# Sliding-window attention and ELU layer on one core: keys cast on load, the band added in PSUM, pairs 2 and 3 ahead of step 0

## The chip, the cores and the metric

The kernel runs on one core of one Trainium2 chip. The metric is the device time of one execution in microseconds: 305.26 us before the change, the median of three executions (304.96 to 305.6). The profiled execution spans 303.4 us, from the first to the last instruction. All times in the text are counted from that span's start.

A core has five engines that run side by side, each its own list of instructions in order: TensorE (PE, with its weight loads shown as PEld), VectorE (DVE), ScalarE (ACT), GpSimd (POOL) and SyncE (SP). POOL, ACT and SP also issue the transfers between memories.

## The reference

Attention over a window of 32 positions on each side, then a layer with ELU. The shapes are 8 batches, 8 heads, 576 positions, 64 values a head; the layer goes 512 to 2048 to 512 over 4608 tokens.

```python
def _attn_ref(q, k, v):
    scale = 1.0 / np.sqrt(D)
    scores = scale * np.matmul(q, k.transpose(0, 1, 3, 2))
    mask = np.abs(pos[:, None] - pos[None, :]) <= 32
    scores = np.where(mask, scores, -1000000000.0)
    scores = scores - np.max(scores, axis=-1, keepdims=True)
    attn = np.exp(scores)
    attn = attn / (np.sum(attn, axis=-1, keepdims=True) + 1e-09)
    return np.matmul(attn, v)

def _moe_ref(x, w_in, w_out):
    h = x @ w_in
    g = np.where(h > 0.0, h, np.exp(np.minimum(h, 0.0)) - 1.0)
    return g @ w_out
```

The attention's result, with the heads side by side, is `x`. Inputs and output are float32; the kernel works in bfloat16 with float32 sums.

## The kernel before

Attention goes by *pairs*: two blocks of 64 queries, all 8 heads, each block against 128 keys. There are 36 pairs. The layer goes by *steps*: 256 tokens by 256 of the 2048 hidden columns, 144 steps; step kk multiplies by `w_in` (`mm1`), takes the ELU, and multiplies by `w_out` (`mm2`) some steps later. Four pairs give the tokens of steps 0 to 7, and so on; from step 0 on, the pairs' work is put between the steps at fixed places.

Loads of the first batch. `load_qk` brings q or k as float32 over the queues of SP and ACT, and a cast to bfloat16 follows on VectorE. `load_cast` brings them over POOL's queue as bfloat16. Each half (HALF_A, HALF_B) has half of each head's positions in it.

```python
def load_qk(b, which, part, engs=(nc.sync, nc.sync)):
    t = lpool.tile([128, 2, nj * D], FP32, tag=f"f{which}{nj}", name=f"f{which}")
    ...
    for h in range(2):
        engs[h].dma_start(out=t[:, h, :], in_=src[:, :, h, :])

def load_cast(b, which, part):
    t = cpool.tile([128, 2, nj * D], BF16, tag=f"c{which}", name=f"c{which}")
    ...                                    # cpool has one buffer for each tag
    for h in range(2):
        nc.gpsimd.dma_start(out=t[:, h, :], in_=src[:, :, h, :])

def load_v(b, m):                          # block m of 128 keys, all heads, as bfloat16
    lo = 128 * m - WIN
    p0 = max(0, -lo)
    p1 = min(128, S - lo)
    nc.gpsimd.dma_start(
        out=V_e[b % 3][p0:p1, m, :, 0:D],
        in_=v[b, :, lo + p0:lo + p1, :].rearrange("h p d -> p h d"))

def rotate_v(b, m0, m1, parts=(0, 1)):     # V_o: the same rows, moved by 64
    e, o = V_e[b % 3], V_o[b % 3]
    for z in parts:
        nc.vector.tensor_copy(o[64 * z:64 * (z + 1), m0:m1],
                              e[64 * (1 - z):64 * (2 - z), m0 + z:m1 + z])

def load_w_in(c): ...                      # a quarter of w_in, POOL's queue
def load_w_out(c): ...                     # a quarter of w_out, POOL's queue
```

Quarter c of `w_in` serves four steps that use columns 512c to 512c+511. The attention of one pair:

```python
def scores(i, tag="s"):
    psS = ps_tile([128, 2, 512], FP32, tag, "psS")
    for z in range(2):
        ...
        for h in range(H):
            nc.tensor.matmul(
                psS[:, h % 2, hp * 128 + z * QB:hp * 128 + (z + 1) * QB],
                lhsT=kT[...], rhs=qT[...], start=True, stop=True)

def exponential(i):                        # ScalarE
    nc.scalar.activation(pu, psS, AX.Exp, scale=SCALE)

def mask(i):                               # VectorE
    nc.vector.tensor_mul(pm, pu, masks)    # masks: ones in the band, zeros outside

def pv(i): ...                             # 16 products pm x V_e or V_o
def normalize(i): ...                      # VectorE: reciprocal and product
def x_transpose(i): ...                    # TensorE
def x_evac(i, eng): ...                    # copy to xT
```

The start of the program (cut; `idle(n, tag)` is n matrix products of zeros, which fill TensorE's waits):

```python
for which in range(2):
    load_qk(0, which, HALF_A, (nc.sync, nc.scalar))
...
edges(0); edges(1)                         # VectorE memsets of the borders of V and k
masks = ...                                # POOL: memset and two selects
for m in (1, 0, 2):
    load_v(0, m)
...
for which in range(2):
    load_cast(0, which, HALF_B)
load_w_in(0)
...                                        # three more selects on masks
for m in (3, 4):
    load_v(0, m)
load_w_in(1)
load_w_out(0)
load_w_out(1)

idle(10, "y1")
front_cast(0, HALF_A, nc.vector)
front_transpose(0, HALF_A, nc.scalar, ("h0", "h1"))
idle(1, "u")
front_cast(1, HALF_A, nc.vector)
for (j0, n), tag, eng in zip(SPLIT, ("y0", "y1"), (nc.scalar, nc.vector)):
    transpose_qk(0, 1, HALF_A, j0, n, eng, tag)
idle(2, "h0")
for i, tag in ((0, "s"), (1, "u")):
    scores(i, tag)
    exponential(i)
idle(4, "y0")
rotate_v(0, 0, 2)
for i in (0, 1):
    mask(i)
pv(0)
front_transpose(0, HALF_B, nc.scalar, ("h0", "h1"))
pv(1)
for i in (0, 1):
    normalize(i)
x_transpose(0); x_evac(0, nc.scalar)
front_transpose(1, HALF_B, nc.vector, ("y0", "y1"))
x_transpose(1); x_evac(1, nc.scalar)
idle(3, "h1")
...                                        # loads of batch 1 and the other quarters
```

The steps. `psH` has two buffers, h0 and h1, so the `mm1` of step kk waits until the ELU of step kk-2 has read its buffer:

```python
def mm1(kk):
    ...                                    # 16 products into psum h0 or h1
    nc.scalar.activation(e_sb, ps, AX.Exp)
    if kk in (1, 2):
        nc.scalar.activation(m_sb, e_sb, AX.Copy, bias=-1.0)
    else:
        nc.vector.tensor_scalar(m_sb, e_sb, -1.0, None, ALU.add)

def elu(kk): ...                           # VectorE: g_sb = min(max(ps, 0), m_sb)

for kk in range(NSTEP + LAG):
    run(kk, "first")
    if 1 <= kk < NSTEP:
        elu(kk - 1)
    run(kk, "dve")
    if kk < NSTEP:
        mm1(kk)
    run(kk, "mid")
    for n in {2: (), 3: (), 4: (), 5: (2, 3)}.get(
            kk, (kk - LAG,) if kk >= LAG else ()):
        mm2(n)                             # cut: the last steps differ
    run(kk, "end")
```

Of the kernel before, what the change touches and what calls it, by code (L numbers as in the profile page):

```python
# [12 lines left out]
ALU = mybir.AluOpType  # L13
# [8 lines left out]
def kernel(  # L22
# [71 lines left out]
    def ps_tile(shape, dt, tag, name):  # L94
        return pools[tag].tile(shape, dt, tag=tag, name=name)
# [32 lines left out]
    def load_cast(b, which, part):  # L128
        z, nj = part
        t = cpool.tile([128, 2, nj * D], BF16, tag=f"c{which}",  # L130
                       name=f"c{which}")
        qk_c[b, which, z] = t
        src = (q, k)[which][b, :, z * NC * nj:(z + 1) * NC * nj, :].rearrange(
            "(g h) (c j) d -> c g h (j d)", h=2, j=nj)
        for h in range(2):
            nc.gpsimd.dma_start(out=t[:, h, :], in_=src[:, :, h, :])  # L136

    def load_v(b, m):
        lo = 128 * m - WIN
        p0 = max(0, -lo)  # L140
        p1 = min(128, S - lo)
        nc.gpsimd.dma_start(  # L142
            out=V_e[b % 3][p0:p1, m, :, 0:D],
            in_=v[b, :, lo + p0:lo + p1, :].rearrange("h p d -> p h d"))
# [28 lines left out]
    def load_w_in(c):  # L173
        w = D_FF // 4
        nc.gpsimd.dma_start(
            out=w_in_sb[:, :, c * w:(c + 1) * w],
            in_=moe_w_in[:, c * w:(c + 1) * w].rearrange(
                "(o p) f -> p o f", p=128))

    def load_w_out(c):  # L180
        n = NFO // 4
        nc.gpsimd.dma_start(
            out=w_out_sb[:, c * n:(c + 1) * n, :],
            in_=moe_w_out[c * n * 128:(c + 1) * n * 128, :].rearrange(
                "(o p) f -> p o f", p=128))
# [1 line left out]
    def w_in_at(c):  # L187
        return w_in_sb[0:1, 0, (c + 1) * (D_FF // 4) - 1:(c + 1) * (D_FF // 4)]

    for which in range(2):  # L190
        load_qk(0, which, HALF_A, (nc.sync, nc.scalar))

    zeros = cpool.tile([128, 512], BF16, name="zeros")
    nc.vector.memset(zeros, 0.0)  # L194
# [11 lines left out]
    make_identity(nc, ident)  # L206

    edges(0)
    edges(1)

    masks = cpool.tile([128, 5, QB], BF16, name="masks")
    nc.gpsimd.memset(masks, 1.0)
    nc.gpsimd.affine_select(
        out=masks, in_=masks, compare_op=ALU.is_ge, fill=0.0,
        base=0, pattern=[[0, 5], [-1, QB]], channel_multiplier=1)
    nc.gpsimd.affine_select(
        out=masks, in_=masks, compare_op=ALU.is_ge, fill=0.0,
        base=2 * WIN, pattern=[[0, 5], [1, QB]], channel_multiplier=-1)  # L220
    for m in (1, 0, 2):
        load_v(0, m)
    kinds = ["FE", "EE", "EL", "LF"]

    def kind(jb):
# [67 lines left out]
            later.append(evict)  # L293

    st = {}

    def scores(i, tag="s"):
        psS = ps_tile([128, 2, 512], FP32, tag, "psS")
        for z in range(2):
            jb = 2 * i + z  # L300
            b, qb = jb // NQB, jb % NQB
            for h in range(H):
                hp, base = h // 2, 64 * (h % 2)
                nc.tensor.matmul(  # L304
                    psS[:, h % 2, hp * 128 + z * QB:hp * 128 + (z + 1) * QB],
                    lhsT=kT[b % 2][base:base + 64, KPAD + hp * S + QB * qb - WIN:
                                   KPAD + hp * S + QB * qb - WIN + 128],
                    rhs=qT[b % 2][base:base + 64, hp, QB * qb:QB * (qb + 1)],
                    start=True, stop=True)
        st[i] = [psS, None, None, None, tag]  # L310

    def exponential(i):
        psS = st[i][0]
        pu = apool.tile([128, H, 2 * QB], BF16, tag="pu")
        nc.scalar.activation(  # L315
            pu, _bap(psS, [psS.ap[0], [1, 1024]]), AX.Exp, scale=SCALE)
        st[i][1] = pu

    def mask(i):
        psS, pu, _, _, _ = st[i]  # L320
        pm = apool.tile([128, H, 2 * QB], BF16, tag="pm")
        m0 = kinds.index(kind(2 * i) + kind(2 * i + 1))
        mm = masks[:, m0:m0 + 2, :]
        nc.vector.tensor_mul(  # L324
            pm, pu, _bap(mm, [mm.ap[0], [0, H], [1, 2 * QB]]))
        st[i][2] = pm
# [42 lines left out]
    def x_evac(i, eng=nc.vector):  # L369
        copy_on(eng, xT_of(i), st.pop(i))  # L370
# [12 lines left out]
    def front_cast(which, part, eng):  # L383
        for j0, n in SPLIT:
            cast_qk(0, which, part, j0, n, eng)

    def front_transpose(which, part, evac, tags, later=None):
        for (j0, n), tag in zip(SPLIT, tags):
            transpose_qk(0, which, part, j0, n, evac, tag, later)


    def idle(n, tag):
        ps = ps_tile([128, 512], FP32, tag, "ps_idle")
        for _ in range(n):
            nc.tensor.matmul(ps, lhsT=zeros[:, 0:128], rhs=zeros,  # L395
                             start=True, stop=True)
# [5 lines left out]

    for which in range(2):
        load_cast(0, which, HALF_B)
    load_w_in(0)
    for mi in (0, 4):
        nc.gpsimd.affine_select(
            out=masks[:, mi, :], in_=masks[:, mi, :], compare_op=ALU.is_ge,
            fill=0.0, base=-WIN, pattern=[[0, QB]], channel_multiplier=1)
    nc.gpsimd.affine_select(  # L410
        out=masks[:, 3, :], in_=masks[:, 3, :], compare_op=ALU.is_ge,
        fill=0.0, base=128 - WIN - 1, pattern=[[0, QB]],
        channel_multiplier=-1)
    for m in (3, 4):
        load_v(0, m)
    load_w_in(1)
    load_w_out(0)
    load_w_out(1)

    idle(10, "y1")  # L420
    front_cast(0, HALF_A, nc.vector)
    front_transpose(0, HALF_A, nc.scalar, ("h0", "h1"))
    idle(1, "u")
    front_cast(1, HALF_A, nc.vector)
    for (j0, n), tag, eng in zip(SPLIT, ("y0", "y1"), (nc.scalar, nc.vector)):
        transpose_qk(0, 1, HALF_A, j0, n, eng, tag)
    idle(2, "h0")
    for i, tag in ((0, "s"), (1, "u")):
        scores(i, tag)
        exponential(i)  # L430
    idle(4, "y0")
    rotate_v(0, 0, 2)
    for i in (0, 1):
        mask(i)
    pv(0)
    front_transpose(0, HALF_B, nc.scalar, ("h0", "h1"))
    pv(1)
    for i in (0, 1):
        normalize(i)
    x_transpose(0)  # L440
    x_evac(0, nc.scalar)
    front_transpose(1, HALF_B, nc.vector, ("y0", "y1"))
    x_transpose(1)
    x_evac(1, nc.scalar)
    idle(3, "h1")


    for which in range(2):
        load_cast(1, which, HALF_A)
# [32 lines left out]
        at(kk + 2, "end", x_evac, i, nc.scalar)  # L482


    at(0, "mid", scores, 2, "s")
    at(0, "mid", scores, 3, "u")
    for i in (2, 3):
        at(0, "mid", exponential, i)
    at(0, "mid", rotate_v, 0, 2, VS - 1, (0,))
    at(0, "mid", mask, 2)  # L490
    at(0, "mid", rotate_v, 0, 2, VS - 1, (1,))
    at(1, "dve", mask, 3)

    at(1, "mid", idle, 4, "y1")
    at(1, "mid", pv, 2)
    at(1, "mid", idle, 2, "y1")
    at(2, "dve", normalize, 2)
    at(2, "mid", pv, 3)
    at(2, "mid", normalize, 3)
    for i in (2, 3):  # L500
        at(3, "mid", x_transpose, i)
        at(3, "mid", x_evac, i, nc.scalar)
        at(3, "mid", lambda n: mm2(n), i - 2)
    at(4, "dve", swap_pools)

    for part, kq in ((HALF_A, 7), (HALF_B, 15)):
# [171 lines left out]
            mm1(kk)  # L678
        run(kk, "mid")

        for n in {2: (), 3: (), 4: (), 5: (2, 3)}.get(
                kk, (kk - LAG,) if kk >= LAG else ()):

            if n < NSTEP - 2:
                mm2(n)
            elif n == NSTEP - 1:
                mm2(n - 1, ((0, 0), (0, 1), (1, 0)))
                mm2(n, ((0, 0), (0, 1)))
                mm2(n - 1, ((1, 1),))
                mm2(n, ((1, 0), (1, 1)))  # L690
        run(kk, "end")
# [30 lines left out]
```

The softmax here doesn't subtract the row's maximum and nothing guards it: scores larger than these inputs give would overflow.

## Time and profile before

| | before |
|---|---|
| time, median of 3 | 305.26 us |
| span of the profiled execution | 303.4 us |
| TensorE busy | 291.2 us, 96% |
| VectorE busy | 241.6 us, 80% |
| ScalarE busy | 169.7 us, 56% |
| first product of step 0 starts | 15.42 us |
| first quarter of w_in: issued, landed | 7.75, 15.37 us |

How to read it: "busy" is time in which an engine has an instruction under way. The chain of waits is followed back from the last instruction, at each step to what released it. A line such as L607 is a line of the kernel's file; L607 is `mm1`, L644 `mm2`, L304 the scores, L336 the values, L324 the mask product, L614 the exponential of the ELU, L631 the ELU, L142, L136 and L175 the loads of V, of cast q and k, and of w_in. A transfer has two times: the slice on the engine that issues it, and its landing, when its semaphore is complete.

### The profile page before, as it was taken

The page shows a single profiled execution, that of the slowest core. Times are in us where ns is not written, and L with a number is a line of the kernel's source. Part 1 is how long each engine was busy: PE and PEld are TensorE (multiplying, and loading weights), DVE is VectorE, ACT ScalarE, POOL GpSimd, SP SyncE. Part 2 cuts the span into 40 slices and gives each one's busy share as a digit, 9 for nine tenths or more (in the row PEclk, how much of TensorE's full clock was granted, in tenths as well). Part 3 has the DMA queues.
Part 4 walks back from the last instruction along what each step waited for, and adds up shares of the span by engine and source line. Part 5 has one row for each costly group of instructions (what it writes and reads, how often), then busy time and mean ns, then how long its engine had stood idle before and what let it go on. Part 6 is the DMA issues. An engine that isn't in the chain of part 4 may idle for free.

```text
span 303.4 us, 7587 instructions
## 1 busy us (share of the span) xinstructions
PE 291.2 (96%) x3037; PEld 197.0 (65%) x3090; DVE 241.6 (80%) x472; ACT 169.7 (56%) x255; POOL 48.6 (16%) x68
## 2 busy tenths in 40 slices
PE   6799999999999999999999999999999999999994
PEld 2466667676666666666666666666666666666662
DVE  6877588978787988888798879887988787877664
ACT  3664657778664566546654675467535353533331
POOL 8836101720004000320023002300000000000000
PEclk9999999999999999999999999999999999999999
DMA  9999999999766978999799969996811111121011
GB/s 190 180 204 205 189 277 412 299 152 222 152 205 150 285 111 237 229 304 143 159 263 319 174 163 264 324 161 157 264 35 71 35 71 35 72 37 69 2 69 70
DMA packets 92117, 52.81 MB, mean 174 GB/s; under 512 B 76594, under 2 KB 81970, under 8 KB 92082
## 3 DMA queue, kind: packets, MB, share of 16 engines
q1 hardware_dynamic: 47330, 35.61, 43.7%
q0 software_dynamic: 42880, 10.10, 41.6%
q10 hardware_dynamic: 1872, 6.62, 5.6%
q8 instruction: 24, 0.39, 0.5%
q14 instruction: 11, 0.09, 0.1%
HBM read 36.70 MB, written 15.34 MB: 172 GB/s over the span
## 4 chain that ended last, share of the span: by engine, by line
PE 89%; DMA 3%; POOL 2%; DVE 2%; issue 2%; ACT 1%; POOLq 0%; DVEq 0%; ACTq 0%
PE ps L607 41%; PE psY L644 40%; PE psS L336 4%; PE psS L304 3%; DMA w_in_sb<-in_moe_w_in_dram 3%; PE ptx L279 1%; POOL Ve L142 1%; POOL c L136 1%; PE psXT L357 1%; ACT pu L315 1%; DVE pm L324 0%; DVE g_sb L631 0%; PE ptx L274 0%; DVE Vo L153 0%; DVE x_st L348 0%
## 5 line engine op out<-in xcount | busy, mean ns | idle before, releaser
L614 ACT ACTIVATE e_sb<-ps 128x512 f32<-128x512 f32 (+1 forms) x145 | 86.4, 596 | 118.4 <-PE ps L607 110.7
L607 PE MATMUL ps<-xT,w_in_sb 128*128 128x256 bf16 x1152 | 149.3, 273 | 0.6 <-DMA w_in_sb<-in_moe_w_in_dram 0.6
L644 PE MATMUL psY<-w_out_sb,g_sb 128*128 128x512 bf16 x526 | 139.4, 379 | 3.1 <-issue 0.8
L607 PEld LDWEIGHTS <-w_in_sb 128*128 128x128 bf16 x1152 | 110.7, 98 | 39.0 <-DMA w_in_sb<-in_moe_w_in_dram 1.1
L631 DVE SCALAR_TENSOR_TENSOR g_sb<-ps,m_sb 128x512 bf16<-128x512 f32 (+1 forms) x145 | 99.5, 686 | 13.0 <-DVE m_sb L620 0.5
L620 DVE TENSOR_SCALAR m_sb<-e_sb 128x512 bf16<-128x512 f32 (+1 forms) x143 | 61.9, 433 | 37.7 <-ACT e_sb L614 35.8
L644 PEld LDWEIGHTS <-g_sb 128*128 128x128 bf16 x576 | 54.5, 98 | 38.5 <-DVE g_sb L631 0.4
L142 POOL DMA_DIRECT2D Ve<-in_v_dram x40 | 35.5, 897 | 139.0 <-PE psS L336 79.9
L315 ACT ACTIVATE pu<-psS 128x1024 bf16<-128x1024 f32 x36 | 36.5, 1020 | 1.5 <-PE psS L304 1.5
L348 DVE TENSOR_TENSOR x_st<-psS,rc 128x512 bf16<-128x512 f32 x36 | 24.9, 692 | 1.2
L324 DVE TENSOR_TENSOR pm<-pu,masks 128x1024 bf16<-128x1024 bf16 x36 | 24.6, 683 | 0.8 <-ACT pu L315 0.6
L234 ACT CAST qkb<-f 128x768 bf16<-128x768 f32 (+1 forms) x29 | 25.0, 861 | 0.0
L336 PEld LDWEIGHTS <-pm 128*64 128x64 bf16 x576 | 11.1, 110 | 9.6 <-DVE pm L324 8.1
L336 PE MATMUL psS<-Ve,pm 128*64 128x65 bf16 x320 | 13.6, 196 | 0.8 <-DVE pm L324 0.7
L236 DVE COPY y_sb<-psY 128x512 f32<-128x512 f32 (+1 forms) x19 | 12.7, 671 | 0.8 <-PE psY L644 0.8
L304 PEld LDWEIGHTS <-kT 64*128 64x128 bf16 x576 | 9.6, 95 | 4.9 <-issue 4.0
L336 PE MATMUL psS<-Vo,pm 128*64 128x65 bf16 x256 | 12.0, 196 | 0.2 <-DVE Vo L153 0.2
L304 PE MATMUL psS<-qT,kT 64*128 64x64 bf16 x576 | 11.8, 191 | 0.5 <-DVE kT L236 0.5
L234 ACT COPY y_sb<-psY 128x512 f32<-128x512 f32 (+1 forms) x18 | 10.3, 571 | 2.8 <-DVE y_sb L236 2.8
L153 DVE COPY Vo<-Ve 64x1040 bf16<-64x1040 bf16 x24 | 10.5, 438 | 1.1 <-DMA Ve<-in_v_dram 0.3
L234 ACT COPY qT<-ptx 128x1152 bf16<-128x1152 bf16 (+2 forms) x8 | 7.6, 975 | 3.5 <-PE ptx L279 2.8
L395 PE MATMUL ps_idle<-zeros 128*128 128x512 bf16 x23 | 7.8, 450 | 1.4 <-DVE zeros L194 1.3
(36 smaller groups left out, 72.2 us busy)
## 6 DMA issues: line engine op xcount, KB each, us to landing
out_dram<-y_sb SPq DMA_DIRECT2D x35, 256.0 KB, 3.9
f<-in_q_dram SPq DMA_DIRECT2D x12, 576.0 KB, 5.7
f<-in_k_dram SPq DMA_DIRECT2D x12, 576.0 KB, 8.3
in_dram<-qkb ACTq DMA_DIRECT2D x10, 576.0 KB, 4.5
Ve<-in_v_dram POOLq DMA_DIRECT2D x24, 128.0 KB, 11.6
w_in_sb<-in_moe_w_in_dram POOLq DMA_DIRECT2D x4, 512.0 KB, 9.8
w_out_sb<-in_moe_w_out_dram POOLq DMA_DIRECT2D x4, 512.0 KB, 12.6
Ve<-in_v_dram POOLq DMA_DIRECT2D x16, 96.0 KB, 10.5
```

Source lines behind the costliest of these rows:

```text
L142: nc.gpsimd.dma_start(out=V_e[b % 3][p0:p1, m, :, 0:D], in_=v[b, :, lo + p0:lo + p1, :].rearrange("h p d -> p h d"))
L234: nc.scalar.copy(d_, s_)
L304: nc.tensor.matmul(psS[:, h % 2, hp * 128 + z * QB:hp * 128 + (z + 1) * QB], lhsT=kT[b % 2][base:base + 64, KPAD + hp * S + QB * qb - WIN: ...
L315: nc.scalar.activation(pu, _bap(psS, [psS.ap[0], [1, 1024]]), AX.Exp, scale=SCALE)
L324: nc.vector.tensor_mul(pm, pu, _bap(mm, [mm.ap[0], [0, H], [1, 2 * QB]]))
L336: nc.tensor.matmul(psS[QB * z:QB * (z + 1), par, hp * VD:(hp + 1) * VD], lhsT=pm[:, par * HP + hp, z * QB:(z + 1) * QB], rhs=vv[:, qb // 2 ...
L348: nc.vector.tensor_mul(x_st, _bap(psS, [psS.ap[0], [VD, HP], [512, 2], [1, D]]), _bap(rc, [rc.ap[0], [2, HP], [1, 2], [0, D]]))
L607: nc.tensor.matmul(ps[:, j, :], lhsT=w_in_sb[:, do, fo * 128:(fo + 1) * 128], rhs=xT[t][:, :, do, :], start=(do == 0), stop=(do == NDO - 1))
L614: nc.scalar.activation(e_sb, ps, AX.Exp)
L620: nc.vector.tensor_scalar(m_sb, e_sb, -1.0, None, ALU.add)
L631: nc.vector.scalar_tensor_tensor(g_t[kk][:, z * w:(z + 1) * w, :], ps, 0.0, m_t[kk][z], ALU.max, ALU.min)
L644: nc.tensor.matmul(psY[t][ts], lhsT=g_t[kk][:, j, ts * 128:(ts + 1) * 128], rhs=w_out_sb[:, s * FG + j, :], start=(s == 0 and j == 0), sto ...
```

## The change

Three things are done at once, all in the start of the program.

- The first half of k comes over POOL's queue as bfloat16 (`load_cast`), as the second half already did, and needs no cast on VectorE.
- For pairs 0 to 3 the band isn't multiplied in after the exponential. A tile `far` holds 0 in the band and -30000 outside. Two products of the identity with `far` lay it into the two PSUM banks of the pair, and the scores are added to it, so that the exponential gives zero outside the band. `masks`, needed from pair 4 on, is made later.
- Scores, exponentials, values and normalization of pairs 2 and 3 stand ahead of step 0; only their transposes stay, in steps 0 and 1. Their V blocks come ahead of w_in, two of them in halves. The `mm2` of steps 0 to 5 are put later: steps 4, 5, 6 (two) and 7 (two).

```diff
-    for which in range(2):
-        load_qk(0, which, HALF_A, (nc.sync, nc.scalar))
+    load_qk(0, 0, HALF_A, (nc.sync, nc.scalar))
+    load_cast(0, 1, HALF_A)
 ...
     edges(0)
-    edges(1)
+    LOW, HIGH = (0, 64), (64, 128)
+    load_v(0, 1)
+    load_v(0, 0)
+    load_v(0, 2, LOW)
+    FAR = -30000.0
+    far = cpool.tile([128, 2, QB], BF16, name="far")
+    nc.vector.memset(far, 0.0)
+    ...                       # three affine_selects on far (POOL)
-    ...                       # memset and two selects of masks
-    for m in (1, 0, 2):
-        load_v(0, m)
+    def make_masks(): ...     # memset and all five selects of masks
 ...
+    MASKED_BY_PE = 4
     def scores(i, tag="s"):
+        masked = i < MASKED_BY_PE
         psS = ps_tile([128, 2, 512], FP32, tag, "psS")
+        if masked:
+            z0 = 0 if i == 0 else 1
+            for par in range(2):
+                nc.tensor.matmul(<bank par of psS>, lhsT=ident,
+                                 rhs=<far, repeated>, start=True, stop=False)
 ...
-                    start=True, stop=True)
+                    start=not masked,
+                    stop=not masked or (z == 1 and h >= H - 2))
 ...
     for which in range(2):
         load_cast(0, which, HALF_B)
+    load_v(0, 2, HIGH)
+    load_v(0, 3)
+    load_v(0, 4, LOW)
     load_w_in(0)
-    ...                       # three selects of masks
-    for m in (3, 4):
-        load_v(0, m)
     load_w_in(1)
     load_w_out(0)
+    load_v(0, 4, HIGH)
     load_w_out(1)
+    make_masks()

     idle(10, "y1")
     front_cast(0, HALF_A, nc.vector)
     front_transpose(0, HALF_A, nc.scalar, ("h0", "h1"))
+    edges(1)
     idle(1, "u")
-    front_cast(1, HALF_A, nc.vector)
     <transposes of k, half A>
-    idle(2, "h0")
     <scores and exponentials of pairs 0, 1>
     idle(4, "y0")
     rotate_v(0, 0, 2)
-    for i in (0, 1):
-        mask(i)
     pv(0)
-    front_transpose(0, HALF_B, nc.scalar, ("h0", "h1"))
     pv(1)
+    front_transpose(0, HALF_B, nc.scalar, ("h0", "h1"), later := [])
+    later.pop(0)()            # eviction of its first part
     for i in (0, 1):
         normalize(i)
     x_transpose(0)
     x_evac(0, nc.scalar)
+    later.pop(0)()            # eviction of its second part
     front_transpose(1, HALF_B, nc.vector, ("y0", "y1"))
     x_transpose(1)
     x_evac(1, nc.scalar)
+    rotate_v(0, 2, VS - 1)
+    for i, tag in ((2, "s"), (3, "u")):
+        scores(i, tag)
+        exponential(i)
     idle(3, "h1")
+    for i in (2, 3):
+        pv(i)
+        normalize(i)
+    idle(2, "h1")
 ...
-    <scores, exponentials, masks, values and normalization of pairs 2, 3
-     in steps 0 to 2, with 4 + 2 idle products in step 1>
     for i in (2, 3):
-        at(3, "mid", x_transpose, i)
-        at(3, "mid", x_evac, i, nc.scalar)
-        at(3, "mid", lambda n: mm2(n), i - 2)
+        at(i - 2, "mid", x_transpose, i)
+        at(i - 2, "mid", x_evac, i, nc.scalar)
 ...
-        for n in {2: (), 3: (), 4: (), 5: (2, 3)}.get(
+        for n in {2: (), 3: (), 4: (0,), 5: (1,), 6: (2, 3), 7: (4, 5)}.get(
```

More of the change, by code (lines that the diff above doesn't have):

```diff
@@ L136, in load_cast, with load_v @@
             nc.gpsimd.dma_start(out=t[:, h, :], in_=src[:, :, h, :])
-    def load_v(b, m):
+    def load_v(b, m, rows=(0, 128)):
         lo = 128 * m - WIN
-        p0 = max(0, -lo)
-        p1 = min(128, S - lo)
+        p0 = max(rows[0], -lo)
+        p1 = min(rows[1], S - lo)
         nc.gpsimd.dma_start(
@@ L208, with make_masks @@
     edges(0)
-    edges(1)
-    masks = cpool.tile([128, 5, QB], BF16, name="masks")
[L214 to L220, printed above, removed]
-    for m in (1, 0, 2):
-        load_v(0, m)
+    LOW, HIGH = (0, 64), (64, 128)
[5 more added lines that the diff above has]
+    nc.vector.memset(far, 0.0)
+    nc.gpsimd.affine_select(
+        out=far, in_=far, compare_op=ALU.is_ge, fill=FAR,
+        base=0, pattern=[[0, 2], [-1, QB]], channel_multiplier=1)
+    nc.gpsimd.affine_select(
+        out=far, in_=far, compare_op=ALU.is_ge, fill=FAR,
+        base=2 * WIN, pattern=[[0, 2], [1, QB]], channel_multiplier=-1)
+    nc.gpsimd.affine_select(
+        out=far[:, 0, :], in_=far[:, 0, :], compare_op=ALU.is_ge, fill=FAR,
+        base=-WIN, pattern=[[0, QB]], channel_multiplier=1)
+    masks = cpool.tile([128, 5, QB], BF16, name="masks")
+    def make_masks():
+        nc.gpsimd.memset(masks, 1.0)
+        nc.gpsimd.affine_select(
+            out=masks, in_=masks, compare_op=ALU.is_ge, fill=0.0,
+            base=0, pattern=[[0, 5], [-1, QB]], channel_multiplier=1)
+        nc.gpsimd.affine_select(
+            out=masks, in_=masks, compare_op=ALU.is_ge, fill=0.0,
+            base=2 * WIN, pattern=[[0, 5], [1, QB]], channel_multiplier=-1)
+        for mi in (0, 4):
+            nc.gpsimd.affine_select(
+                out=masks[:, mi, :], in_=masks[:, mi, :],
+                compare_op=ALU.is_ge, fill=0.0, base=-WIN,
+                pattern=[[0, QB]], channel_multiplier=1)
+        nc.gpsimd.affine_select(
+            out=masks[:, 3, :], in_=masks[:, 3, :], compare_op=ALU.is_ge,
+            fill=0.0, base=128 - WIN - 1, pattern=[[0, QB]],
+            channel_multiplier=-1)
     kinds = ["FE", "EE", "EL", "LF"]
@@ L295 @@
     st = {}
+    MASKED_BY_PE = 4
     def scores(i, tag="s"):
+        masked = i < MASKED_BY_PE
         psS = ps_tile([128, 2, 512], FP32, tag, "psS")
+        if masked:
+            z0 = 0 if i == 0 else 1
+            for par in range(2):
+                nc.tensor.matmul(
+                    _bap(psS, [psS.ap[0], [128, HP], [QB, 2], [1, QB]],
+                         par * 512),
+                    lhsT=ident,
+                    rhs=_bap(far, [far.ap[0], [0, HP], [QB * (1 - z0), 2],
+                                   [1, QB]], z0 * QB),
+                    start=True, stop=False)
         for z in range(2):
@@ L316, in exponential @@
             pu, _bap(psS, [psS.ap[0], [1, 1024]]), AX.Exp, scale=SCALE)
-        st[i][1] = pu
+        st[i][2 if i < MASKED_BY_PE else 1] = pu
     def mask(i):
@@ L404 @@
         load_cast(0, which, HALF_B)
+    load_v(0, 2, HIGH)
+    load_v(0, 3)
+    load_v(0, 4, LOW)
     load_w_in(0)
[L406 to L413, printed above, removed]
-    for m in (3, 4):
-        load_v(0, m)
     load_w_in(1)
     load_w_out(0)
+    load_v(0, 4, HIGH)
     load_w_out(1)
+    make_masks()
     idle(10, "y1")
@@ L482, in pair_at @@
         at(kk + 2, "end", x_evac, i, nc.scalar)
-    at(0, "mid", scores, 2, "s")
-    at(0, "mid", scores, 3, "u")
     for i in (2, 3):
[L488 to L500, printed above, removed]
-        at(3, "mid", x_transpose, i)
-        at(3, "mid", x_evac, i, nc.scalar)
-        at(3, "mid", lambda n: mm2(n), i - 2)
+        at(i - 2, "mid", x_transpose, i)
+        at(i - 2, "mid", x_evac, i, nc.scalar)
     at(4, "dve", swap_pools)
```

## The prediction

> **What bounds the kernel now.** I read the page first, then the windows by stage, then the chain in order of time for the first 30 us, then the timeline and the landing of each transfer. From the page:
>
> ```profile
> span 303.4 us, 7587 instructions
> PE 291.2 (96%) x3037; PEld 197.0 (65%) x3090; DVE 241.6 (80%) x472; ACT 169.7 (56%) x255; POOL 48.6 (16%) x68
> PEclk9999999999999999999999999999999999999999
> ```
>
> TensorE is busy nearly all the time, at full clock throughout. So only its work and its holes count. The windows (columns: stretch, length, then busy time and instructions of PE, PEld, DVE, ACT, POOL) tell where the holes are:
>
> ```profile
> 0.00:15.40 15.40, 10.70 (x144) 5.60 (x146) 11.21 (x26) 8.08 (x11) 13.30 (x27) 1.00 1.24 186
> 15.40:44.40 29.00, 28.21 (x319) 19.23 (x325) 20.93 (x41) 16.58 (x25) 8.57 (x11) 1.00 1.39 212
> 50.00:100.00 50.00, 49.26 (x566) 34.77 (x573) 41.19 (x79) 34.83 (x50) 13.35 (x15) 1.00 1.29 215
> ```
>
> From 15.4 us on, TensorE has almost no hole (28.21 of 29.00, then 49.26 of 50.00). A start that comes sooner by one microsecond, or one microsecond of filler taken out after it, is one microsecond off the end. Everything the change touches lies before about 30 us. What ends the start is in the chain (start, length, what):
>
> ```profile
> 2.78 2.62 POOL Ve L142 x3
> 5.41 2.34 POOL c L136 x4
> 7.75 7.63 DMA w_in_sb<-in_moe_w_in_dram
> 15.37 0.05 issue
> 15.42 1.06 PE ps L607 x8
> ```
>
> The reader is to see one queue: POOL issues V, then q and k, then the first quarter of w_in, and step 0 waits for that quarter to land (15.37). After it the timeline of TensorE shows steps 1 to 3 thinned by the attention of pairs 2 and 3:
>
> ```profile
> 16.97 1.05 PE L607 MATMUL ps<-xT,w_in_sb 128*128 128x256 bf16 x8
> 18.07 0.81 PE L395 MATMUL ps_idle<-zeros 128*128 128x512 bf16 x3
> 20.05 1.04 PE L607 MATMUL ps<-xT,w_in_sb 128*128 128x256 bf16 x8
> 21.39 1.05 PE L607 MATMUL ps<-xT,w_in_sb 128*128 128x256 bf16 x8
> 32.13 1.04 PE L607 MATMUL ps<-xT,w_in_sb 128*128 128x256 bf16 x8
> ```
>
> These are the first products of steps 1, 2, 3 and 8. Step 8 starts 16.71 us after step 0. I use its start as the finishing post: in both kernels the same matrix products lie behind it (first products of steps 0 to 7, second products of 0 to 5), and the program after it is unchanged.
>
> **What the Trainium skill says.** (1) "DMA: Bandwidth & Descriptors", section "Issuing engines are not separate DMA queues": transfers started by different engines run on the same 16 DMA engines and interleave. So moving k from two hardware queues to POOL's queue doesn't make k free. The trace fits: the queue table shows q0 and q1 each taking about 42% of 16 engines. (2) "Perfetto Trace Analysis", section "DMA Instruction — SWDGE (GPSIMD)": a POOL DMA slice ends when the descriptors are written, not when the data are there. The trace agrees: 0.78 us of slice, 7.63 us from issue to landing for that quarter of w_in. I therefore read landings, not slices. (3) "PSUM — Partial Sum Buffer", section "The four PSUM rules": a matmul with the start flag clears the bank's written bits, and later ones without it add where the bit is set. That is what lets an identity product lay the band into a bank and the scores add to it. No run here shows it yet.
>
> **Part 1, keys cast on the way in.** VectorE loses two casts of k (0.92 us, 6.54 to 7.46). Before, k landed at 5.67 and 6.52 us. POOL's two k transfers now go first, at 0.8 us. A c transfer took about 4.8 us to land, so k is there by 5.7 in any case. TensorE does 18 half transposes (0.67 us) for 9 whole ones (0.74). VectorE gets the memsets of batch 1's edges (four, about 1.7 us) between the q cast and the k eviction, so the eviction still ends near 8.3 (8.67 before). Gain on the first scores: 0.4 us.
>
> **Part 2, bands by TensorE.** Four products with the mask (0.69 us each, VectorE) go; eight 512-column products come, at about 0.22 us each by the spacing of the idle products. Two of them replace the two idle products ahead of pair 0. On the chain of pairs 0 and 1 this takes out one mask and its handover, 0.75 us. Values of pair 0 are then ready to start near 10.1, not 11.14.
>
> **Part 3, POOL's queue.** This decides. Issue: k 0.8 to 2.0 (2 x 0.58); identity to 2.6; V block 1 still at 2.7 (its memset on VectorE ends at 2.68); blocks 1, 0 and half of 2 to 5.0 (1.01, 0.79, 0.5); three selects of the new band tile to 6.0 (the 128x128 select took 0.29 each, plus gaps). So the second halves of q and k are issued at 6.0, where before it was 5.38: 0.6 later. Their last landing was 12.36; I put it at 12.9. Then, newly ahead of w_in: half of block 2, block 3 and half of block 4, 2048 rows of 64 values. Landings of V blocks in the full queue were 0.67 to 1.08 us apart, so about 2 us. Then 2.5 to 3.0 us for the quarter of w_in (w_in 1 to w_out 0 and w_out 0 to w_out 1 were both 2.52 apart; w_in 0 came 3.01 after the last c). Sum: 12.9 + 2.0 + 2.7 = 17.6 us for w_in 0, instead of 15.37. Later quarters move only by some 0.5 us (w_out 0 near 22.7 instead of 22.25), since the same V rows stood behind w_in 0 before.
>
> **Part 4, pairs 2 and 3 ahead of step 0.** Their keys land at 12.9; the first eviction starts 0.5 later and two take 1.45 us: 14.85. Scores 0.4, two exponentials 2.05 (1.02 each), values 0.5: 17.8. With the two idle products about 18.2. This chain and w_in 0 end together. I take S = 17.6 for step 0, the landing.
>
> **The ramp.** Steps 0 to 3 now have only first products, and a PSUM buffer of two (h0, h1), so they go at the pace of the ELU chain. From S: ACT starts exponential 0 at 1.08 (15.42 to 16.50 before). ACT's order is e0, copy x(2), e1, m1, copy x(3), e2, m2: five at 0.60, two at 0.63, seven gaps of 0.03, that is 4.5, so it ends at S+5.5. ELU 2 on VectorE takes 0.69 and the handover 0.1, so step 4 starts at S+6.3. From there TensorE is full: four first products at 0.87, six second ones at 0.86, transposes of batch 1 at 0.62, that is 9.3. Step 8 at S+15.6. TensorE's work in this is 13.2, so 2.4 us of new holes stand where scores, values and idle products stood. The ramp shortens by 16.7 - 15.6 = 1.1 us; the start moves back by 17.6 - 15.4 = 2.2 us. Sum: +1.1 us. I shade it to +0.9, because the idle products at the end of the new prologue only make sense if pairs 2 and 3 are done before w_in, which would mean a quicker chain than mine. Predicted: 305.26 + 0.9 = 306.2 us.
>
> **Rivals.** (A) *The idle time at the start is filled for nothing.* Step 0 would still find w_in near 15.5 to 16.4, because the queue starts at 0.8 instead of 2.7, and the ramp gains its 1.1: 304.2 to 305.2 us. For it: DMA did nothing in the first 2 us. Against it: 256 more k packets and 1536 more V packets stand ahead of w_in, and the gap before the second q and k is not used. (B) *The chain of pairs 2 and 3 becomes the bound*, not w_in: keys landing at 13.4, step 0 at 18.6, hence 307.4. For it: the second k load reuses the first one's buffer and must wait for its transposes, near 7.1, and everything on POOL behind it waits too. (C) *The ramp fills better than I think*, because buffers come free a little earlier: 0.5 us less. (D) A colder TensorE clock: fewer idle products (20 instead of 26). Against it: the clock was 1.00 in every stretch, and the new prologue has more real work in it. I give it little.
>
> **Range and chances.** S may be 16.5 (A) to 18.6 (B), the ramp is good to 0.7 us. Together 304.2 to 308.0 holds most of it. Two per cent is 6.1 us; the whole region touched is 30 us with a few us of slack, so neither side is likely to get there: faster 0.01, same 0.97, slower 0.02.
>
> **What would show each step.** The chain after should still hold the w_in landing or, in rival B, ACT pu and PE psS right before step 0. First product at 17.6 (15.4 before); w_in 0 landing 2 us after the last V ahead of it; steps 2, 3 and 4 started 3.0, 4.4 and 6.3 us after step 0 with VectorE's g_sb as what TensorE waited for; no mask product before 30 us; from step 8 on, the same distance to the end. The prediction is wrong if w_in lands before 16.5, if steps 1 to 4 follow without holes, or if a later wait (w_in 2, batch 1's q and k) appears.

## The result and the profile after

The changed kernel takes 307.83 us (median; 307.69 to 308.05) against 305.38 us for the kernel before: a ratio of 1.0083, with a 95% interval of 1.0069 to 1.0097. It is slower by 2.45 us. The prediction was 306.2 us in a range of 304.2 to 308.0, so the time lies in the range, near its upper end, and the loss is more than twice the predicted one.

The page after, its first lines:

```profile
span 306.0 us, 7617 instructions
PE 292.5 (96%) x3049; PEld 197.4 (65%) x3101; DVE 238.0 (78%) x467; ACT 169.5 (55%) x255; POOL 51.8 (17%) x75
```

TensorE's busy time grew by 1.3 us and VectorE's fell by 3.6, as the change means it to be. The windows by stage (columns as before) show where the time is lost:

```profile
15.40:44.40 29.00, 26.49 (x291) 17.82 (x295) 18.20 (x35) 15.08 (x22) 11.08 (x18) 1.00 1.42 197
50.00:100.00 50.00, 49.21 (x572) 34.98 (x581) 41.18 (x81) 35.20 (x50) 11.86 (x14) 1.00 1.33 223
```

In the second stage TensorE is busy for 26.49 of 29.00 us, where it was 28.21. In the steady part it is the same (49.21 of 50.00 and 49.26). So the loss is in the start. TensorE's timeline after shows the first products of steps 0 to 4 and of step 8; the brackets tell how long TensorE was idle before them and what ended it:

```profile
18.98 1.04 PE L632 MATMUL ps<-xT,w_in_sb 128*128 128x256 bf16 x8
20.08 1.04 PE L632 MATMUL ps<-xT,w_in_sb 128*128 128x256 bf16 x8
21.97 1.03 PE L632 MATMUL ps<-xT,w_in_sb 128*128 128x256 bf16 x8 [0.63 <-DVE g_sb L656]
23.19 1.03 PE L632 MATMUL ps<-xT,w_in_sb 128*128 128x256 bf16 x8 [0.18 <-DVE g_sb L656]
25.07 1.03 PE L632 MATMUL ps<-xT,w_in_sb 128*128 128x256 bf16 x8 [0.85 <-DVE g_sb L656]
...
34.47 1.04 PE L632 MATMUL ps<-xT,w_in_sb 128*128 128x256 bf16 x8
```

Step 0 starts at 18.98 instead of 15.42: +3.56 us. Step 8 starts 15.49 us after it instead of 16.71: -1.22 us. From step 8 to the end it is 271.5 us, and was 271.3. Together +2.6 us, the difference of the two spans. What step 0 waits for is in the chain after:

```profile
8.27 5.33 DMA c<-in_k_dram
13.64 0.48 PE ptx L301 x9
14.15 1.46 DVE kT L263 x2
15.65 0.43 PE psS L343 x16
16.17 0.83 ACT pu L355
17.09 1.03 ACT pu L355
18.16 0.45 PE psS L376 x16
18.61 0.54 PE ps_idle L435 x2
19.14 0.89 PE ps L632 x8
```

The landing of w_in has left the chain. The last transfer of the second half of k lands at 13.60, and from it on each piece waits for the one before it: transposes, two evictions, scores of pair 2, two exponentials, values of pair 3, two idle products, step 0. But w_in is close: its first quarter landed at 18.35, and the values of pair 3 ended at 18.61. The two things that step 0 needs came out 0.3 us apart. POOL's own timeline tells why both are late:

```profile
1.32 1.25 POOL L136 DMA_DIRECT2D c<-in_k_dram  x2 [0.81 <-POOLq L731]
3.10 2.56 POOL L142 DMA_DIRECT2D Ve<-in_v_dram  x3
6.64 1.12 POOL L136 DMA_DIRECT2D c<-in_q_dram  x2
7.75 1.09 POOL L136 DMA_DIRECT2D c<-in_k_dram  x2
8.79 2.32 POOL L142 DMA_DIRECT2D Ve<-in_v_dram  x3
11.05 1.56 POOL L175 DMA_DIRECT2D w_in_sb<-in_moe_w_in_dram  x2
```

The second halves of q and k are issued at 6.64 instead of 5.38, w_in at 11.05 instead of 7.75.

### The profile page after: what moved, and what is told of

Its sections match the earlier page's. It is cut to its first block, busy times and chain, and to the rows that moved or that the text cites. A ratio compares the mean times of both kernels' runs of the same rounds, so it can differ in the third digit from the quotient of the medians.

```text
span 306.0 us, 7617 instructions
## 1 busy us (share of the span) xinstructions
PE 292.5 (96%) x3049; PEld 197.4 (65%) x3101; DVE 238.0 (78%) x467; ACT 169.5 (55%) x255; POOL 51.8 (17%) x75
## 4 chain that ended last, share of the span: by engine, by line
PE 88%; DVE 3%; issue 2%; ACT 2%; POOL 2%; DMA 2%; DVEq 0%; POOLq 0%; ACTq 0%
PE ps L632 40%; PE psY L669 39%; PE psS L376 3%; PE psS L343 3%; DMA c<-in_k_dram 2%; PE ptx L306 1%; ACT pu L355 1%; DVE g_sb L656 1%; POOL c L136 1%; ACT e_sb L639 1%; POOL Ve L142 1%; PE ptx L301 1%; PE psXT L397 1%; DVE kT L263 0%; DVE m_sb L645 0%
## 5 line engine op out<-in xcount | busy, mean ns | idle before, releaser
L142 POOL DMA_DIRECT2D Ve<-in_v_dram x42 | 36.5, 881 | 136.6 <-PE psS L376 79.9
L364 DVE TENSOR_TENSOR pm<-pu,masks 128x1024 bf16<-128x1024 bf16 x32 | 21.8, 681 | 0.5 <-ACT pu L355 0.5
L376 PEld LDWEIGHTS <-pm 128*64 128x64 bf16 x512 | 9.6, 110 | 7.3 <-DVE pm L364 6.5
L376 PE MATMUL psS<-Ve,pm 128*64 128x65 bf16 x288 | 11.5, 196 | 0.1
L376 PE MATMUL psS<-Vo,pm 128*64 128x65 bf16 x224 | 10.3, 196 | 0.0
L385 DVE RECIPROCAL rc<-psS 128x8 f32<-128x8 f32 x36 | 7.1, 198 | 2.4 <-PE psS L376 2.4
```

What stands on the lines that cost most here:

```text
L142: nc.gpsimd.dma_start(out=V_e[b % 3][p0:p1, m, :, 0:D], in_=v[b, :, lo + p0:lo + p1, :].rearrange("h p d -> p h d"))
L364: nc.vector.tensor_mul(pm, pu, _bap(mm, [mm.ap[0], [0, H], [1, 2 * QB]]))
L376: nc.tensor.matmul(psS[QB * z:QB * (z + 1), par, hp * VD:(hp + 1) * VD], lhsT=pm[:, par * HP + hp, z * QB:(z + 1) * QB], rhs=vv[:, qb // 2 ...
```

## The experiments

All times below are medians, with the ratio to the kernel before on the same chip (305.2 to 305.4 us) and its 95% interval. "Step 0" and "step 8" are the starts of their first products in the profiled execution. Where a profiled execution took clearly longer than the median, this is said.

**Part 1 alone.** The kernel before, with the first half of k through POOL.

```diff
-    for which in range(2):
-        load_qk(0, which, HALF_A, (nc.sync, nc.scalar))
+    load_qk(0, 0, HALF_A, (nc.sync, nc.scalar))
+    load_cast(0, 1, HALF_A)
 ...
-    front_cast(1, HALF_A, nc.vector)
```

> The kernel before with part 1 alone: first half of k through POOL's queue, no cast on VectorE. My theory (step 0 waits for the first quarter of w_in, whose place in POOL's queue decides): the two k transfers push V, q, k and w_in back on POOL, w_in lands at 15.9 to 16.5 us instead of 15.37, step 0 starts with it, time up by 0.5 to 1.1 us (306.0). The rival (the cast on VectorE was on the path, the queue has room): step 0 at 15.0 to 15.4, time 304.9 to 305.3.

Measured: 307.42 us, ratio 1.0070 (1.0057 to 1.0083), twice the upper end of the loss I expected. V is issued at 4.49 instead of 2.73, since POOL now issues k first (1.32 to 2.55) and makes the identity and the masks after it. w_in landed at 16.79 and step 0 started at 16.84 (+1.4), as the theory has it, somewhat more. The rest was not in my sum. V blocks 3 and 4 landed at 19.46 and 19.87 (before: 16.72 and 17.80), pairs 2 and 3 waited for them within the steps, and step 2 started at 22.12 instead of 20.05. The second quarter of w_in was as late, 21.96 instead of 19.73, and the weights of step 2 waited for it (PEld is their load):

```profile
22.00 0.88 PEld L606 LDWEIGHTS <-w_in_sb 128*128 128x128 bf16 x8 [0.21 <-DMA w_in_sb<-in_moe_w_in_dram]
```

So neither the V blocks nor this quarter can be called the cause alone. Step 8 started at 34.20, 2.1 us late. Each transfer in POOL's queue is later, and more than one of them has a reader waiting.

**Part 2 alone.** Bands by TensorE in the kernel before.

```diff
-    masks = ...; for i in (0, 1): mask(i); idle(2, "h0"); mask 2, 3 in steps 0, 1
+    far = ...               # on POOL, ahead of V, where the masks were
+    MASKED_BY_PE = 4        # scores() lays the band first, as in the change
+    make_masks()            # after load_w_out(1)
```

> The kernel before with part 2 alone: bands of pairs 0 to 3 laid by TensorE, masks made later, pairs 2 and 3 still within steps 0 to 2, V order as before. My theory: w_in still lands near 15.4 and starts step 0; VectorE without the masks of pairs 2 and 3 reaches the ELU of steps 0 and 1 some 0.7 us sooner, TensorE has four more 0.22 us products in step 0; time 304.6 to 305.4. Rival (the band products are the costly part): 306 or more, with step 1 late.

Measured: 305.57 us, ratio 1.0013 (1.0004 to 1.0022). Within 0.2 us of what the theory gave, and no gain. Step 0 started sooner, at 14.91, because w_in was issued at 7.34 and landed at 14.86. Nothing came of it:

```profile
14.91 1.05 PE L634 MATMUL ps<-xT,w_in_sb 128*128 128x256 bf16 x8
17.54 1.05 PE L634 MATMUL ps<-xT,w_in_sb 128*128 128x256 bf16 x8
20.20 1.04 PE L634 MATMUL ps<-xT,w_in_sb 128*128 128x256 bf16 x8
```

These are steps 0, 1 and 2 of that kernel. Step 2 needs the second quarter of w_in, which landed at 20.10; in the kernel before at 19.73, with step 2 at 20.05. But TensorE was not free before that either: between step 0 and step 2 it shows no wait, because the band products now stand there, about 0.5 us for each pair before its scores begin:

```profile
15.79 0.59 PE L330 MATMUL psS<-far,ident 128*128 128x512 bf16 x2
16.32 0.41 PE L342 MATMUL psS<-qT,kT 64*128 64x64 bf16 x16
16.66 0.60 PE L330 MATMUL psS<-far,ident 128*128 128x512 bf16 x2
17.20 0.41 PE L342 MATMUL psS<-qT,kT 64*128 64x64 bf16 x16
```

Step 1 comes 2.63 us after step 0, and was 1.55. So the rival was in part right: the band products cost TensorE about what the sooner start gave, and the landing of w_in stands right behind them. Which of the two holds step 2 isn't told apart here.

**Parts 1 and 2, pairs 2 and 3 back in the steps.** The edits of the two runs above together.

> Parts 1 and 2 together, that is the changed kernel with pairs 2 and 3 back in steps 0 to 2 and V and w_in in the order of before. My theory: moving pairs 2 and 3 ahead of step 0 is the costly part (step 0 at 18.98 instead of 15.42), so most of the 2.45 us goes: 305.5 to 306.2. Rival (parts 1 and 2 carry the loss): 307 or more.

Measured: 309.14 us, ratio 1.0130 (1.0107 to 1.0153), from 308.23 to 310.77 us; the profiled execution is the slowest of them. My theory said that undoing part 4 takes most of the loss away. It fell: without part 4 the loss is larger. V is issued at 4.32 (3.10 in the changed kernel), w_in lands at 18.63, and step 0 waits 2.5 us for it with nothing to do.

**The changed kernel without part 1.**

```diff
-    load_qk(0, 0, HALF_A, (nc.sync, nc.scalar))
-    load_cast(0, 1, HALF_A)
+    for which in range(2):
+        load_qk(0, which, HALF_A, (nc.sync, nc.scalar))
 ...
     nc.vector.memset(far, 0.0)
+    edges(1)
 ...
-    edges(1)
     idle(1, "u")
+    front_cast(1, HALF_A, nc.vector)
```

> The changed kernel without part 1: first half of k by SP and ACT as float32 with its cast on VectorE; batch 1's edges set before them. My theory: POOL starts V 0.4 us and the second half of k 0.6 to 0.9 us sooner, the chain k eviction, scores 2, 3, exponentials, values moves with it, step 0 at 18.1 to 18.5 instead of 18.98; time 306.9 to 307.4. Rival (the k chain isn't the bound, w_in is, and it is held by the V rows ahead of it): step 0 at 18.9, 307.8.

Measured: 306.89 us, ratio 1.0052 (1.0039 to 1.0064), as expected. V was issued at 1.70 and the second half of k at 6.57; it landed at 11.96 instead of 13.60. Step 0 started at 18.16, step 8 at 33.65: both 0.8 us sooner than in the changed kernel, and the time fell by 0.94. Part 1 costs this much in the changed kernel. The run doesn't say which of the two ends held step 0, for both moved: the values of pair 3 ended at 17.79, and w_in landed at 17.72.

**Parts 1 and 2 with V ahead of the band tile**, against the run of parts 1 and 2.

```diff
+    for m in (1, 0, 2):
+        load_v(0, m)
     FAR = -30000.0
     ...
-    for m in (1, 0, 2):
-        load_v(0, m)
```

> Parts 1 and 2 with pairs 2 and 3 in steps 0 to 2, but now with the V loads ahead of the band tile on POOL, as the changed kernel has them (V issued at 3.1 instead of 4.3 us). Theory now: the two k transfers ahead of everything hold up POOL and its queue, and each microsecond of it reaches w_in and the V blocks of pairs 2, 3. Then w_in lands about 1 us sooner than in the kernel before this one, near 16.8 to 17.6, and the time falls from 309.14 to 307.3 to 308.3. Rival (the place of V doesn't matter, parts 1 and 2 cost by themselves): 309.

Measured: 308.21 us, ratio 1.0105 (1.0069 to 1.0140), from 307.38 to 311.57; the profile is of the 311.57 one. The median is 0.9 us below that of the run of parts 1 and 2, as expected, but the two intervals overlap, so a gain from V's place isn't shown; and w_in landed at 18.41 in the profiled execution, not near 17. This profile shows what a long wait does besides. TensorE's longest wait and then the windows (the third column from the end is the granted clock):

```profile
PE ps L633 <- DMA w_in_sb<-in_moe_w_in_dram: 3.5, 1, 3.5
```

```profile
16.00:18.00 2.00, 0.00 (x0) 0.00 (x0) 0.00 (x0) 0.00 (x0) 1.29 (x4) 0.78 1.63 182
18.00:20.00 2.00, 1.55 (x8) 1.12 (x9) 0.00 (x0) 0.00 (x0) 0.85 (x2) 0.50 1.31 203
20.00:22.00 2.00, 2.00 (x21) 0.80 (x20) 0.93 (x3) 0.76 (x2) 0.95 (x2) 0.50 1.24 206
22.00:24.00 2.00, 2.00 (x23) 1.04 (x22) 1.03 (x2) 1.52 (x2) 0.75 (x1) 0.51 1.24 207
24.00:26.00 2.00, 2.00 (x27) 1.13 (x26) 0.09 (x1) 1.59 (x3) 0.54 (x1) 1.00 1.22 203
```

With 3.5 us without work the clock is 0.50 for 6.83 us, from 17.13 to 23.96, and the products of step 0 take 1.89 us instead of 1.05. The Trainium skill ("TensorE: Matmul & The Clock Gate", section "What's actually happening") says that the clock is halved after an idle window of about 3.4 us, and is full again after a busy window of about as long. The lengths agree: the clock was 0.50 for 6.83 us here, twice 3.41, and for 3.41 us in each of four other variants. The beginning doesn't: it fell 2.2 us after TensorE's last product (14.97), and in the run of parts 1 and 2 after a wait of no more than 2.5 us. In these two profiled executions, each the slowest of its run, parts 1 and 2 without part 4 thus lose twice, by the wait and by the clock after it.

**The changed kernel without the last two idle products.**

```diff
     for i in (2, 3):
         pv(i)
         normalize(i)
-    idle(2, "h1")
```

> The changed kernel without the two idle products ahead of step 0. If the chain of pairs 2 and 3 is what step 0 waits for, step 0 starts as soon as the last value product is through, 0.4 us sooner (18.6), since w_in lands at 18.35: time 307.4 instead of 307.83. If w_in were the bound, step 0 would stay at 19.0 and the time with it.

Measured: 308.41 us, ratio 1.0093 (1.0075 to 1.0111). Inconclusive. Two executions took 307.3 and 307.4 us, which is what the theory asks for; four took 308.2 to 308.9, two of them with a mean clock of 0.992 and 0.994. In the profiled one (308.2) w_in landed at 19.42, though POOL issued the same transfers, up to w_in's first quarter, at the same times to within 0.03 us, and step 0 waited for it:

```profile
19.47 1.05 PE L631 MATMUL ps<-xT,w_in_sb 128*128 128x256 bf16 x8 [0.99 <-DMA w_in_sb<-in_moe_w_in_dram]
```

So neither of the two can be called the only thing that holds step 0: in this execution, with the chain cut by 0.4 us, w_in takes its place at once. Between the profiled executions of the two kernels w_in's landing differs by 1 us.

**Two more PSUM buffers for the ramp.** First products of steps 2 and 3 go to the banks of the output sums.

```diff
+        if kk in (2, 3):
+            tags = (f"y{h}",)
 ...
-        for n in {2: (), 3: (), 4: (0,), 5: (1,), 6: (2, 3), 7: (4, 5)}.get(
+        for n in {2: (), 3: (), 4: (), 5: (0, 1), 6: (2, 3), 7: (4, 5)}.get(
```

> The changed kernel with two more PSUM buffers for the ramp: first products of steps 2 and 3 go to the banks of the output sums (y0, y1), which are free until the first second product, which moves from step 4 to step 5. If the holes of 1.7 us between steps 1 and 4 come from two buffers that wait for the ELU, steps 2 and 3 follow step 1 at once, step 4 starts 4.1 to 4.5 us after step 0 instead of 6.1, and the time falls by 0.6 to 1.1 us to 306.7 to 307.2. If the ELU chain itself (ScalarE and VectorE) sets the pace, step 8 stays 15.5 us after step 0 and the time at 307.8.

Measured: 306.46 us, ratio 1.0042 (1.0028 to 1.0056), 1.4 us below the changed kernel and a little below the expectation.

```profile
18.79 1.04 PE L634 MATMUL ps<-xT,w_in_sb 128*128 128x256 bf16 x8
19.89 1.04 PE L634 MATMUL ps<-xT,w_in_sb 128*128 128x256 bf16 x8
21.02 3.67 PE L634 MATMUL ps<-xT,w_in_sb 128*128 128x256 bf16 x32
...
32.98 1.04 PE L634 MATMUL ps<-xT,w_in_sb 128*128 128x256 bf16 x8
```

The third line is steps 2 to 5 in one piece, without a hole. Step 8 starts 14.19 us after step 0 (15.49 in the changed kernel). The holes came from having two buffers, not from the pace of the engines that do the ELU.

**The three together**: k by hardware queues, no last idle products, the two buffers; the diffs are those above.

> The version that the runs so far point to: the changed kernel with k by hardware queues, without the last two idle products, with the two more ramp buffers. If the three are independent, 306.89 - 0.4 - 0.8 = 305.6 to 305.8, about the kernel before (305.2). It beats the kernel before only if w_in then lands well before 17 us.

Measured: 305.18 us, ratio 0.9999 (0.9991 to 1.0007): the kernel before again, and 2.65 us below the change. The profiled execution is the slowest (306.12): w_in landed at 18.81 and step 0 waited 0.9 us for it.

**w_in ahead of the V blocks of pairs 2 and 3**, in the changed kernel.

```diff
+    load_w_in(0)
     load_v(0, 2, HIGH)
     load_v(0, 3)
     load_v(0, 4, LOW)
-    load_w_in(0)
```

> The changed kernel with the first quarter of w_in ahead of the V blocks of pairs 2 and 3 on POOL, nothing else. If the order of the queue is what matters and pairs 2, 3 stay ahead of step 0, the quarter lands near 16 but the V blocks 2 to 2.5 us later (17 to 19), so values 2 and 3 and with them step 0 come later: step 0 near 19.5, 308.2 to 309. If w_in's landing is the bound (rival), step 0 moves forward and the time falls below 307.4.

Measured: 311.66 us, ratio 1.0213 (1.0193 to 1.0233). The rival is out, and the loss is larger than I expected. w_in landed at 16.79, V blocks at 17.98 to 19.64. TensorE's waits, the longest:

```profile
PE psS L376 <- DVE Vo L153: 2.0, 1, 2.0
...
PE psS L376 <- DMA Ve<-in_v_dram: 1.1, 1, 1.1
```

Values 2 and 3 wait 3.1 us for V, with step 0 behind them (21.29) though its weights have been there for 4.5 us. The clock falls to 0.50 here too (between 22 and 24 us), and step 0 takes 1.91 us.

**A version meant to beat both**: the three together, w_in first, values 2 and 3 after step 1, their transposes ahead of step 2.

```diff
+    load_w_in(0)              # ahead of V 2 HIGH, 3, 4 LOW
-    pv and normalize of pairs 2, 3 ahead of step 0; idle(3, "h1")
+    idle(2, "h1")
+    rotate_v(0, 2, VS - 1) in step 0; pv, normalize in step 1;
+    x_transpose, x_evac ahead of the first product of step 2
```

> A version meant to beat both: the one before this (k by hardware, ramp buffers, no last idle) with w_in's first quarter ahead of V 2 to 4, and values 2 and 3 after the first product of step 1 instead of ahead of step 0, their transposes ahead of step 2. If the start is bound by what the queue has delivered, step 0 starts near 16.2, step 2 with the second quarter near 20, and the six first products are done near 23.7 instead of 24.6: 304.3 to 305.0, below both. If values 2, 3 hold up step 2 instead, 305.2 or more.

Measured: 308.40 us, ratio 1.0100 (1.0084 to 1.0117). It missed. w_in landed at 15.48, but the scores of pairs 2 and 3, still ahead of step 0, ended at 16.58, and step 0 started at 16.95, 0.75 us later than expected. Steps 0 and 1 were then done by 18.9. The values of pair 2 waited 1.0 us for VectorE's rotation of V, and the transposes ahead of step 2 waited 1.3 us (0.89 and 0.44), because VectorE does the rotation, an ELU and two normalizations first. Step 2 started at 22.69, and the clock went to 0.50:

```profile
18.00:20.00 2.00, 1.01 (x9) 0.63 (x8) 1.28 (x3) 1.67 (x3) 1.07 (x2) 1.00 1.25 205
20.00:22.00 2.00, 1.06 (x35) 0.79 (x34) 1.91 (x5) 0.16 (x1) 0.75 (x1) 1.00 1.34 200
22.00:24.00 2.00, 1.56 (x13) 1.22 (x13) 0.99 (x2) 1.17 (x2) 0.35 (x1) 0.77 1.28 211
24.00:26.00 2.00, 2.00 (x11) 1.39 (x10) 0.46 (x1) 1.27 (x3) 1.17 (x2) 0.50 1.20 199
```

Steps 2 to 5 took 5.32 us instead of 3.67. The sooner start was spent waiting.

**The changed kernel without part 2.**

```diff
-    far = ...; MASKED_BY_PE = 4; make_masks() after load_w_out(1)
+    masks = ...             # memset and two selects where far was made,
+                            # three selects after the second halves of q, k
+    idle(2, "h0") ahead of pair 0; mask(0), mask(1) ahead of pv(0);
+    mask(2), mask(3) ahead of pv(2)
```

> The changed kernel without part 2: mask products on VectorE again for pairs 0 to 3, the masks made where the band tile was made (memset and two selects) and after the second halves of q and k (three selects), the two idle products back ahead of pair 0. If step 0 waits for the chain of pairs 2 and 3, one mask product and its handover (0.75 us) and 0.4 us of POOL time add to it: step 0 near 20.0 instead of 18.98, 308.6 to 309.2. So part 2 would be a gain of about 1 us where pairs 2, 3 stand ahead of step 0, though it was none by itself (305.57). Rival (w_in alone sets step 0): time within 0.4 us of 307.83.

Measured: 309.70 us, ratio 1.0144 (1.0128 to 1.0160). That is more than expected. Step 0 is at 19.88, as expected; its products took 1.65 us, with the clock at 0.50 between 18 and 20 us, which I had not counted. Undoing part 2 costs 1.9 us where pairs 2 and 3 stand ahead of step 0, this clock included; by itself part 2 gained nothing. The mask product in the chain to step 0, and the values behind it:

```profile
17.73 0.70 DVE pm L339
18.47 0.65 PE psS L351 x10
```

## Why the prediction was right, and where it was off

**The range and the number.** The time lies in the range because the range reaches to rival B. The number itself was 1.6 us short: a loss of 0.9 us was predicted, 2.45 measured.

**The finishing post.** Right. Nothing behind step 8 changed (271.5 and 271.3 us; 271.2 to 271.6 in every variant), and nearly the whole difference is made before it.

**The ramp.** Right, and the best term: step 2 at S+3.0 (measured 2.99), step 4 at S+6.3 (6.09), step 8 at S+15.6 (15.49), with VectorE's g_sb as what TensorE waits for. The run with two more buffers shows that the cause was the one named.

**The start of step 0.** The term that was mis-sized: 17.6 predicted, 18.98 measured. Of the 1.4 us, 0.7 is the later landing of k, 0.1 the chain behind it, and 0.6 the choice of the wrong end.

- POOL's issues. I let the first k transfer start at 0.8 us; it started at 1.32. I took half a V block for half a slice (0.5 us); the first one took 0.86, nearly as long as a whole block (0.92). So the second halves of q and k were issued at 6.64, not 6.0, and the last landed at 13.60, not 12.9.
- The chain behind it was counted right: from that landing to step 0 I had 5.3 us (12.9 to 18.2), measured 5.38.
- w_in landed at 18.35, 0.75 us later than my 17.6. That it came so near is in part luck: from the last landing of k, the V blocks ahead of it took 3.0 us (13.60 to 16.62) where I had 2.0, and the quarter itself 1.7 us where I had 2.7. The two errors cancel.

And then I chose the earlier of the two ends. My own chain gave 18.2, and I took the 17.6 of w_in. The ramp with S = 18.2 would have given +1.7 us. On top I shaded the sum down, because the idle products seemed to say that pairs 2 and 3 are done before w_in. The measured order is the other way round in the profiled execution, by 0.3 us. So what the prediction named as the last wait, the landing of w_in, isn't what the chain shows: it shows ACT pu and PE psS right before step 0, the sign of rival B (the chain of pairs 2 and 3 is the bound, step 0 at 18.6, 307.4 us). But the reason given for B, a wait for the buffer of the first k load, doesn't show: POOL issues the second half of k at 7.75 right behind q.

**Part 1.** The direction wasn't seen. I credited it with 0.4 us on the first scores, which came (8.31 instead of 8.82), and counted its cost only as a place in the queue. In the changed kernel it costs 0.94 us, and by itself 2.2.

**Part 2.** Its size on the chain of a pair (0.75 us) holds: in the changed kernel without part 2 the mask product with its handovers takes 0.77 us (17.70 to 18.47). Step 0 moved by 0.9 us, with a sooner k landing (13.26) and a slower clock in it as well. That it also relieves POOL, because three selects on a small tile stand ahead of w_in instead of a memset and five selects, was not in my sum as a gain: undone, w_in is issued at 12.99 instead of 11.05 and lands at 19.58 instead of 18.35, and the time lost is 1.9 us in all.

**Parts 3 and 4.** By difference: the changed kernel without part 1 is 1.3 us above part 2 alone (306.89 and 305.57). But they don't simply add. With part 1 and part 2 already in, the time doesn't rise when pairs 2 and 3 move to the front: it was 309.14, or 308.21 with V in the changed kernel's place, and is 307.83. Of these differences, 1.3 us has the move of V in it, and 0.4 us lies inside the spread. The profiles show a reason: where w_in is late anyway, the pairs fill a wait of 2.5 to 3.5 us, and the clock stays at 1.00.

**Rival D, the clock**, got little weight and needed little for this change: the clock was 1.00 through the start. In the profiled executions of five variants it was not.

**Where the expected gain went.** The change takes 3.6 us out of the steps: before, the 7.08 us from step 0 to the first second product (15.42 to 22.50) held four first products of 0.87 us, and the rest was attention, idle products and short waits. Only 1.22 us of it came off the way to step 8. Most of the difference, 1.66 us, is the three waits for g_sb shown above, and the run with two more buffers won back 1.4. The start paid 3.56 us for having the work first.

**What stays open.** The landing of w_in differs by up to 1 us between kernels that issue it at the same time to within 0.1 us (18.35, 18.45, 19.42). Its semaphore gets 16 increments; in the run with V ahead of the band tile, 14 had come by 15.94, one came at 17.18 and the last at 18.41. The Trainium skill ("DMA: Bandwidth & Descriptors", section "Why a DMA increments its semaphore by 16 and not by 1") says that a transfer runs on up to 16 engines which finish independently, and the trace agrees: one late engine is the landing. In that run two single packets took 1.4 to 1.5 us where 0.1 is usual. Why single packets are held up so is open. An instruction fetch, one packet of 16 KB that takes 0.96 to 1.31 us, also starts between 12 and 15 us in each of these profiles; whether it holds up one engine of w_in isn't shown. Open too is how part 1's cost divides: without part 1 the first V block is issued 1.40 us sooner but lands only 0.56 us sooner (7.85 instead of 8.41), so POOL's time and the place among the transfers are not told apart.

## What to carry to other kernels

Work moved ahead of a wait is free only as long as it ends before the wait does; when work and wait end within a fraction of a microsecond of each other, predict with the later of the two, and check who waits for the next transfer in the same queue. In a start that is fed by one issuing queue, count each issue at its measured slice, by transfer rather than by bytes, because the issue of every transfer behind it moves. Interleaved attention was also the filler that let two PSUM buffers be enough: take the filler out, and give the steps more buffers with the same change.

## What the runs showed of the hardware

A V transfer of half the rows (64 of 128) took 0.74 to 0.86 us of POOL's time in the changed kernel, against 0.92 to 0.94 for all of them. The landing of a transfer is that of its slowest engine (one w_in quarter had 14 of 16 increments by 15.94 us and the last at 18.41), and it differed by 1 us between kernels with the same issues (18.35 and 19.42). The clock of TensorE fell to half in the variant with a gap of 3.5 us, but also where TensorE had been busy about half of the time for 4 us (1.01 and 1.06 of 2 us in the version meant to beat both, 1.01 and 1.07 without part 2). In the first of these it cost 1.65 us on four steps.
